# Eight head transposes on SyncE's DMA instead of TensorE, and a new order of steps, in a fused linear-attention and gated-unit kernel

## The chip, the cores and the metric

The kernel runs on one core of one Trainium2 chip. The metric is the device time of one execution in microseconds (us), the median of several executions. The engines are named as the profile names them: PE is TensorE (PEld its weight loads), DVE is VectorE, ACT is ScalarE, POOL is GpSimd, and SP is SyncE, which here only issues DMAs and passes signals on. A name with a q, such as SPq, is the engine's instruction queue.

## What is computed

There are 8 batches of 8 heads, 576 tokens and 64 values per head. Both parts of the reference, cut to what matters:

```python
def phi(x):                                   # w_phi: 64 x 128
    proj = np.einsum('bhsd,df->bhsf', x, w_phi)
    proj = proj - np.max(np.abs(proj), axis=-1, keepdims=True)
    return np.concatenate([np.exp(proj), np.exp(-proj)], axis=-1)
q_p, k_p = phi(q), phi(k)
kv  = np.einsum('bhsf,bhsd->bhfd', k_p, v)
z   = np.sum(k_p, axis=2)
num = np.einsum('bhsf,bhfd->bhsd', q_p, kv)
den = np.einsum('bhsf,bhf->bhs', q_p, z)[..., None] + 1e-06
x   = (num / den).transpose(0, 2, 1, 3).reshape(B, S, 512)

gate_pre = sum(conv_w[k] * x_shifted_by(4 - k) for k in range(5))   # causal, along the tokens
val = x @ moe_w_val
out = (sigmoid(gate_pre) * val) @ moe_w_out
```

## The kernel before

**Units and stages.** The work is cut into 32 units, one for each pair of heads: units 0 to 3 are batch 0, and so on, so that units 20 to 23 are batch 5 and units 24 to 27 batch 6. A partition holds nine neighbouring tokens; eight of them go through the units and the ninth of all four units of a batch through a small extra unit (names that end in e). For one unit, in order:

- T (L347) transposes k and q on PE, Tc copies them out of PSUM; PK and PQA (L360) project them.
- mKa, mKb and mQ (L377, DVE) take the maxima; Ka, Kb (L441, ACT) the exponentials of k, E (L426, ACT) the factors of the maxima; V (L467, L471, POOL) scales v by them, DMQ (L412, POOL) spreads q's maxima.
- PQa and PQb (L534, PE) project q the other way round, in two halves that write one bank from different rows of the array. WQ (L526) is an empty instruction in SP's queue that waits for PQa, and PQb waits for it. SH (L550) subtracts the maxima; Qp and Qm (L564, ACT) are q's exponentials.
- KV (L488, L496, PE) sums over the tokens, KVM copies the sums; NUM (L582, PE) is numerator and denominator, RCP and XN (L597, L602, DVE) divide: XN is 128 tokens x 512 values, in bf16.
- The gated part needs XN transposed. XP (L612, PE) makes four transposes of 128 x 128 into one bank of PSUM, and XC (L152 on ACT, L154 on DVE) copies that bank into XT, the transposed x of the batch.

Once the four units of a batch are in XT, HL (L154, POOL) copies the halo of the convolution inside XT; GA (L796, PE) is the convolution, TH (L828, ACT) the gate, VA (L839) and GV (L860) the value, OUT (L868) the last product, OE (L891 on ACT, L893 on DVE) the copy out of PSUM, ST (L903, SP) the store. Two batches share one ninth-token pass (GAe to STe).

**What sets the order.** Every step is a word of one long string, `ORDER`, for instance `XP21@3` (unit 21, PSUM bank 3) or `XC21:D` (on DVE; A is ACT, P is POOL). A loop walks the string and issues the steps; each engine executes its own instructions strictly in that order, and an instruction that has to wait holds all that follow it on its engine. Semaphores between engines, buffers and DMAs are set by the framework. SP's DMAs use eight completion semaphores in turn, so a DMA on SP also waits until the eighth one before it has landed. Loads of k and q are issued by POOL, loads of v, all stores and the WQ instructions by SP.

**The second way for XC.** Where XC carries no engine letter, the step already knows another form: one DMA on SP's queue that transposes XN and writes XT, without PE, PSUM or a copy.

```python
def crossbar(i):
    u = units[i]
    nc.sync.dma_start_transpose(
        xt(u.b)[:, u.hp, 4 + u.hp % 2:12 + u.hp % 2, :].rearrange("p (j g) t -> p j (g t)", g=2),
        u.XN[:, :, :, :].rearrange("p a x d -> p (a x d)"),
    )
```

In the kernel before no step uses it.

Of the kernel before, what the change touches and what calls it, by code (L numbers as in the profile page):

```python
# [76 lines left out]
ST3_3 LVa7 LVb6 PQb22 SH22 VA4_1@2 GV4_1 Ka24 Qm22 KV22@6 KVM22:D Qp22 NUM21@0 RCP21 mKb24 E24 V24:P OUT4_1@7
PQA25@2 OE4_1:A XN21 STe1 PKe6@4 OUT4_3@0 mQ25 KTe6 OE4_3:A PQea5@6 WQe5 mQe6 DMQe6:P PK25@2,1 PQeb5 SHe5 mKe6
ST3_1 Qe5 KV23@3 T26@0 PQa23@4 WQ23 KVM23:D PQb23 SH23 mKa25 Ee6 Tc26:D Kb25 NUM22@6 RCP22 XP21@3 XN22 Qp23
Qm23 OUT4_0@0 XP22@6 XP20@7 XC21:D OE4_0:A Ka25 mKb25 NUM23@3 OUT4_2@1 DMQ25:P XC20:D RCP23 XC22:D XN23 E25  # L80
PQA26@5 OE4_2:A PK26@2,7 PQa24@3 Ka26 WQ24 NUMe5@0 PQb24 mQ26 DMQ24:P SH24 RCPe5 XNe5 Qm24 Qp24 Te7@1 Tce7:D
XP23@5 Ve6:P T27@6 XC23:D V25:P KV25@0 mKb26 KVM25:A XPe5@5 XCe5:D DMQ26:P HL5:P mKa26 Kb26 KV24@1 KVM24:D E26
V26:P LE7 PQa25@4 WQ25 PQb25 SH25 NUM24@0 Tc27:D RCP24 GA5@2,6 XN24 Qp25 Qm25 THy5 PK27@1,0 mKb27 mKa27
VA5_1@4 THx5 Ka27 NUM25@6 Kb27 VA5_0@5 RCP25 XN25 T28@3 XP24@2 PQA27@6 GV5_0 Tc28:A XP25@5 XC24:D XC25:A
PQa26@1 ST4_1 WQ26 T31@0 PQb26 SH26 Qp26 mQ27 PKe7@6 GV5_1 Qm26 mQe7 mKe7 Tc31:D VA5_2@3 GV5_2 KV26@5 KTe7
VA5_3@4 E27 DMQe7:P T29@2 GV5_3 Tc29:D GAe2@0,6 KVM26:A PK28@5,4 PQa27@2 LVb7 Ee7 ST4_3 THey2 PQA28@6 mKa28
THex2 WQ27 mQ28 DMQ27:P PQb27 SH27 Kb28 T30@0 Tc30:D OUT5_3@1 V27:P NUM26@6 Qp27 Qm27 mKb28 RCP26 Ve7:P Ka28
OUT5_1@0 KV27@2 PQea6@4 WQe6 E28 XN26 KVM27:A PK29@7,3 OE5_1:A PQeb6 SHe6 OE5_3:D mKa29 mKb29 OUT5_2@2 OE5_2:D
Qe6 NUM27@0 RCP27 Kb29 NUMe6@6 PQa28@4 RCPe6 OUT5_0@2 XN27 XP26@0 XNe6 Ka29 XC26:A OE5_0:D XP27@3 DMQ28:P
XPe6@1 XC27:D WQ28 XCe6:A PQA29@6 mQ29 E29 PQb28 SH28 Qm28 PK30@0,2 Qp28 mKb30 Ka30 VAe2@1 GVe2 V28:P KV28@3  # L90
# [932 lines left out]
```

## Time and profile before

| | |
|---|---|
| median of 3 runs | 221.36 us (219.36 to 221.43) |
| profiled execution, its own time | 220.76 us |
| its span | 219.0 us, 8941 instructions |
| granted PE clock over the span | 0.981 |
| PE busy | 201.0 us, 92% |
| ACT busy | 193.7 us, 88% |
| DVE busy | 188.0 us, 86% |
| POOL busy | 149.9 us, 68% |
| moved by DMA | 32.40 MB, mean 148 GB/s |

The span runs from the first to the last instruction that the profile shows; the time has 1.8 us more around it. Busy times count computing instructions alone. In a row of the timeline the first number is the start, the second how long the merged group took, and a bracket at the end says how long the engine had been idle and what released it. Instructions of one engine overlap a little, so what a step costs its engine is the distance from its start to the start of the next one, not its own length.

### The profile page before, as it was taken

How to read it: one execution, taken by the hardware profiler on the slowest of the kernel's cores; microseconds unless marked ns; L12 is line 12 of the kernel's file. 1: busy time of each engine (PE TensorE's matmuls, PEld its weight loads, DVE VectorE, ACT ScalarE, POOL GpSimd, SP SyncE). 2: the span in 40 equal slices, each digit the busy share in tenths (PEclk: the TensorE clock that was granted, in tenths of full speed). 3: DMA queues.
4: the chain of work that ended last, by engine and by line, in shares of the span. 5: the costliest groups of instructions: out<-in, count | busy, mean ns of one | idle time of the engine just before them, and what ended most of it. 6: DMA issues, size and time to landing. Idle time of an engine off the chain costs nothing.

```text
span 219.0 us, 8941 instructions
## 1 busy us (share of the span) xinstructions
PE 201.0 (92%) x3755; PEld 134.6 (61%) x3788; DVE 188.0 (86%) x339; ACT 193.7 (88%) x386; POOL 149.9 (68%) x180
## 2 busy tenths in 40 slices
PE   7676989979999999999999999999999999999991
PEld 2443758647676676766676668655576667656640
DVE  6786999989999999989989999898998999876362
ACT  3599899998999999999999999799999999988450
POOL 8969968999676498986864768595881695840000
PEclk9969699999999999999999999999999999999998
DMA  6999995069989912999980794719922800404726
GB/s 168 231 256 209 242 218 122 4 136 203 246 183 177 236 34 48 158 226 253 256 201 3 138 196 103 152 31 216 240 49 76 207 15 1 102 18 128 187 57 192
DMA packets 28194, 32.40 MB, mean 148 GB/s; under 512 B 6005, under 2 KB 23285, under 8 KB 28154
## 3 DMA queue, kind: packets, MB, share of 16 engines
q1 hardware_dynamic: 18282, 20.79, 38.7%
q0 software_dynamic: 9328, 10.19, 28.8%
q10 hardware_dynamic: 544, 0.85, 1.2%
q8 instruction: 29, 0.48, 0.9%
q14 instruction: 11, 0.09, 0.2%
HBM read 32.58 MB, written 9.44 MB: 192 GB/s over the span
## 4 chain that ended last, share of the span: by engine, by line
PE 67%; DMA 7%; POOL 6%; issue 5%; DVE 5%; ACT 4%; SPq 3%; POOLq 0%; DVEq 0%; ACTq 0%
PE PS L868 11%; PE PS L839 8%; DMA kN<-in_k_dram 7%; PE PS L496 7%; PE PS L582 6%; PE PS L347 5%; PE PS L360 5%; PE PS L612 4%; PE PS L534 4%; PE PS L796 3%; PE PS L550 3%; PE PS L488 2%; ACT KT L441 2%; PE PS L948 2%; POOL VT L467 2%
## 5 line engine op out<-in xcount | busy, mean ns | idle before, releaser
L467 POOL TENSOR_TENSOR VT<-vN,E 128x1024 bf16<-128x1024 f32 x32 | 61.0, 1905 | 23.3 <-ACT E L426 23.0
L441 ACT ACTIVATE KT<-PS 128x512 bf16<-128x512 f32 x128 | 69.2, 640 | 1.7 <-PE PS L360 0.9
L564 ACT ACTIVATE QT<-PS 128x1024 bf16<-128x1024 f32 x64 | 62.4, 1056 | 1.7 <-PE PS L550 1.4
L377 DVE TENSOR_REDUCE MK<-PS 128x4 f32<-128x512 f32 x64 | 42.6, 682 | 2.9 <-PE PS L360 2.2
L377 DVE TENSOR_REDUCE MQ<-PS 128x8 bf16<-128x1024 f32 x32 | 39.1, 1221 | 4.4 <-PE PS L360 3.8
L412 POOL TENSOR_TENSOR DM<-id,MQ 128x512 bf16<-128x512 bf16 x32 | 33.1, 1040 | 11.7 <-DVE MQ L377 11.4
L868 PE MATMUL PS<-WOUT,GV 128*128 128x512 bf16 x113 | 30.2, 379 | 1.2 <-issue 0.6
L839 PE MATMUL PS<-XT,WVAL 128*128 128x512 bf16 x115 | 29.9, 379 | 0.8 <-issue 0.2
L360 PE MATMUL PS<-W,T 64*128 64x128 bf16 x512 | 24.8, 222 | 2.1 <-ACT T L152 1.1
L496 PE MATMUL PS<-VT,KT 128*128 128x65 bf16 x512 | 24.0, 196 | 0.0
L860 DVE SCALAR_TENSOR_TENSOR GV<-GATE,PS 128x512 bf16<-128x512 bf16 x32 | 21.1, 682 | 3.4 <-ACT GATE L823 2.1
L360 PEld LDWEIGHTS <-T 64*128 64x128 bf16 x512 | 17.6, 97 | 9.1 <-issue 4.0
L602 DVE TENSOR_TENSOR XN<-PS,RCP 128x512 bf16<-128x512 f32 x32 | 21.9, 687 | 0.7
L496 PEld LDWEIGHTS <-KT 128*128 128x128 bf16 x512 | 21.7, 99 | 0.9
L582 PEld LDWEIGHTS <-QT 128*128 128x128 bf16 x512 | 18.4, 97 | 4.8 <-issue 2.4
L582 PE MATMUL PS<-KVS,QT 128*128 128x65 bf16 x512 | 20.8, 193 | 0.0
L534 PE MATMUL PS<-T,W 64*128 64x256 bf16 x128 | 17.8, 281 | 2.5 <-SPq L526 1.2
L154 DVE COPY T<-PS 128x1024 bf16<-128x1024 bf16 x27 | 18.2, 682 | 1.8 <-PE PS L347 1.8
L467 POOL TENSOR_TENSOR VZ<-vE,Ee 64x512 bf16<-64x512 f32 x16 | 16.6, 1039 | 2.9 <-ACT Ee L426 2.3
L839 PEld LDWEIGHTS <-WVAL 128*128 128x128 bf16 x128 | 11.2, 98 | 11.7 <-issue 0.9
L868 PEld LDWEIGHTS <-GV 128*128 128x128 bf16 x128 | 10.8, 98 | 10.8 <-issue 1.3
L488 PE MATMUL PS<-VZ,KTe 128*128 128x130 bf16 x64 | 14.3, 223 | 0.1
(92 smaller groups left out, 365.0 us busy)
## 6 DMA issues: line engine op xcount, KB each, us to landing
vN<-in_v_dram SPq DMA_DIRECT2D x32, 320.0 KB, 7.0
out_dram<-OS SPq DMA_DIRECT2D x28, 256.0 KB, 4.1
qN<-in_q_dram POOLq DMA_DIRECT2D x7, 576.0 KB, 11.4
kN<-in_k_dram POOLq DMA_DIRECT2D x7, 576.0 KB, 10.3
vE<-in_v_dram SPq DMA_DIRECT2D x16, 64.0 KB, 6.4
out_dram<-OSe SPq DMA_DIRECT2D x8, 128.0 KB, 4.8
GV<-in_moe_w_val_dram POOLq DMA_DIRECT2D x1, 512.0 KB, 16.0
WOUT<-in_moe_w_out_dram POOLq DMA_DIRECT2D x4, 128.0 KB, 13.6
```

The source lines that it names most:

```text
L360: (nc.tensor.matmul(PS[:, banks[g], jj * F:(jj + 1) * F], T[row(g), n, jj, :, :].rearrange("p a t -> p (a t)"), W2[row(g), :], start=True, ...
L377: nc.vector.tensor_reduce(dst, x, AX.X, ALU.max, apply_absolute_value=True)
L412: engines[eng].tensor_tensor(u.DM[:, :, :], id64[:, :].unsqueeze(1).to_broadcast([P, n, 64]), u.MQ[:, :, :].rearrange("p j g -> p (j g)"). ...
L441: nc.scalar.activation(u.KT[:, ft, par, :, :].rearrange("p b f -> p (b f)"), PS[:, u.PK[par], :], AF.Exp, scale=1.0 if ft == 0 else -1.0,)
L467: engines[eng].tensor_tensor(dst[:, :, :, 0:D].rearrange("p f (h m) d -> p f h m d", m=m), x.unsqueeze(1).to_broadcast(s), e.rearrange("p ...
L496: nc.tensor.matmul(o, u.KT[:, ft, y % 2, h2 * 2 + y // 2, :], u.VT[:, ft, h2 * 4 + y, :], start=False, stop=(y == 3), skip_group_check=True,)
L534: return nc.tensor.matmul(PS[:, u.PQ + a, :].rearrange("p (j g t) -> p g j t", g=2, t=64)[:, g, :, :], W2[row(g), :], u.T[row(g), 1, :, a, :],
L564: nc.scalar.activation(u.QT[:, ft, :, :, :].rearrange("p a n t -> p a (n t)"), half(u.PQ, 512), AF.Exp, scale=1.0 if ft == 0 else -1.0,)
L582: (nc.tensor.matmul(u.NUM[:, jj // 2, x * E1:(x + 1) * E1], u.QT[:, ft, jj // 2, 4 * h2 + 2 * (jj % 2):4 * h2 + 2 * (jj % 2) + 2, :].rearr ...
L602: nc.vector.tensor_tensor(u.XN[:, :, :, :], numview(u)[:, :, :, 0:D], u.RCP[:, :, :].unsqueeze(3).to_broadcast([P, 2, 4, D]), ALU.mult,)
L839: nc.tensor.matmul(PS[:, m.val[r], :], WVAL[:, dt, r, :], xt(b)[:, dt, 4:12, :].rearrange("p n t -> p (n t)"), start=(dt == 0), stop=(dt = ...
L868: nc.tensor.matmul(PS[:, m.out[j], :], m.GV[:, r, j * P:(j + 1) * P], WOUT[:, r, :], start=(r == 0), stop=(r == 3),)
```

## The change

The only edit is the string ORDER. Three things differ in it.

1. Eight steps are gone, XP20 to XP27, and the eight steps XC20 to XC27 have lost their engine letter (six were on DVE: 20 to 24 and 27; two on ACT: 25 and 26). Units 20 to 27, batches 5 and 6, thus get into XT by SP's DMA. The other 24 units keep XP and XC.
2. The whole string is written in another order, with other PSUM banks, from the first loads to the last stores.
3. Some copies have another engine. On ACT there are three more KVM (13 to 16) and three more OE (18 to 21), and fewer Tc (5 to 3), Tce (3 to 2), XC (9 to 6) and XCe (1 to 0). On DVE there are three fewer KVM (19 to 16), three fewer OE (14 to 11), two more Tc (27 to 29), one more Tce (5 to 6), five fewer XC (23 to 18) and one more XCe (7 to 8). At the start one ZV (two memsets) goes from DVE to ACT and ND from DVE to POOL; at the end HLa7 goes from ACT to POOL.

Since string and banks differ nearly everywhere, two lines of the diff show its kind:

```diff
-PQA25@2 OE4_1:A XN21 STe1 PKe6@4 OUT4_3@0 mQ25 KTe6 OE4_3:A PQea5@6 WQe5 mQe6 DMQe6:P PK25@2,1 PQeb5 SHe5 mKe6
-ST3_1 Qe5 KV23@3 T26@0 PQa23@4 WQ23 KVM23:D PQb23 SH23 mKa25 Ee6 Tc26:D Kb25 NUM22@6 RCP22 XP21@3 XN22 Qp23
...
+DMQ23:P SH23 NUM22@4 mKb25 XC21 Qp23 RCP22 XN22 V23:P E25 KV23@0 KVM23:D OUT4_2@1 OE4_2:D T26@5 Qm23 NUM23@2
+XC22 Tc26:D OUT4_0@0 V24:P Kb25 RCP23 XN23 XC23 Te7@1 PK26@7,5 PQa24@3 Ka25 Tce7:D NUMe5@6 mKa26 RCPe5 XNe5
```

Three places of the program show what moves. (Lines of the changed kernel are one lower than before.)

**SP's queue around batches 5 and 6.** vN and vE are buffers of v, OS and OSe the outputs, XT_129 the x of batches 4 and 5, XT_131 that of 6 and 7. Before, from batch 3's last stores to batch 5's (the vN pair is the last load of v):

```order
L903 DMA out_dram<-OS 64x2x512 x2
L297 DMA vE<-in_v_dram 128x2x64 x2
L903 DMA out_dram<-OS 64x2x512 x2
L292 DMA vN<-in_v_dram 64x4x320 x2
L903 DMA out_dram<-OS 64x2x512 x6
```

After, the same place:

```order
L902 DMA out_dram<-OS 64x2x512 x2
L977 DMA out_dram<-OSe 64x512 x2
L618 DMA_TRANSPOSE XT_129<-XN 128x4x128 x3
L618 DMA_TRANSPOSE XT_131<-XN 128x4x128 x2
L291 DMA vN<-in_v_dram 64x4x320 x2
L902 DMA out_dram<-OS 64x2x512 x4
L618 DMA_TRANSPOSE XT_131<-XN 128x4x128
L902 DMA out_dram<-OS 64x2x512 x2
L618 DMA_TRANSPOSE XT_131<-XN 128x4x128
```

Seven of the eight transposes stand here, between loads and stores (the eighth, unit 20's, is some DMAs earlier). Each waits in the queue for its XN on DVE, and for the DMA eight places before it. The WQ instructions, which these lists leave out, stand among them: WQ24 right behind the transposes of units 21, 22 and 23, WQ27 behind those of 24 and 25 and two loads, WQ29 behind that of unit 27 and two stores.

**DVE in batch 5.** MK is a maximum, XN the divided result, T the transposed k and q, KVS the sums. Before, from unit 22's division to the copies of batch 5:

```order
L597 RECIPROCAL RCP<-PS 128x8
L602 TENSOR_TENSOR XN<-PS,RCP 128x512
L154 COPY XT_129<-PS 128x512
L377 TENSOR_REDUCE MK<-PS 128x4
L154 COPY XT_129<-PS 128x512
L597 RECIPROCAL RCP<-PS 128x8
L154 COPY XT_129<-PS 128x512
L602 TENSOR_TENSOR XN<-PS,RCP 128x512
```

After, from the same division on:

```order
L596 RECIPROCAL RCP<-PS 128x8
L601 TENSOR_TENSOR XN<-PS,RCP 128x512
L153 CAST KVS<-PS 128x260
L892 TENSOR_SCALAR OS<-PS 128x512
L153 COPY T<-PS 128x1024
L596 RECIPROCAL RCP<-PS 128x8
L601 TENSOR_TENSOR XN<-PS,RCP 128x512
```

The three copies into XT are gone from between the divisions of units 22 and 23, and other copies stand there.

**POOL before the convolution of batch 5.** VT is scaled v, DM the spread maxima; the COPY of XT_129 onto itself is HL5. What an instruction waits for is in its bracket (DMAHW: a DMA issued by SP). Before:

```order
L467 TENSOR_TENSOR VT<-vN,E 128x16x64 [waits Activation_49,Pool_49]
L471 CAST VT<-E 128x16
L412 TENSOR_TENSOR DM<-id_138,MQ 128x512 [waits DVE_49]
L154 COPY XT_129<-XT_129 128x4x4x63 [waits DVE_49]
L467 TENSOR_TENSOR VT<-vN,E 128x16x64 [waits DMAHW7_49,DMAHW0_49,Activation_49]
```

After:

```order
L411 TENSOR_TENSOR DM<-id_138,MQ 128x512 [waits DVE_49,Pool_49]
L466 TENSOR_TENSOR VT<-vN,E 128x16x64 [waits Activation_49]
L470 CAST VT<-E 128x16
L153 COPY XT_129<-XT_129 128x4x4x63 [waits DMAHW2_49,DMAHW1_49,DMAHW5_49,DMAHW0_49,DVE_49]
L411 TENSOR_TENSOR DM<-id_138,MQ 128x512 [waits DVE_49]
L466 TENSOR_TENSOR VT<-vN,E 128x16x64 [waits DMAHW3_49,Activation_49]
```

HL5 now waits for the four DMA transposes of its batch; behind it on POOL are the spread maxima and the scaled v of unit 26. HL6 stands the same way in batch 6.

More of the change, by code (lines that the diff above doesn't have):

```diff
@@ L79 @@
-ST3_1 Qe5 KV23@3 T26@0 PQa23@4 WQ23 KVM23:D PQb23 SH23 mKa25 Ee6 Tc26:D Kb25 NUM22@6 RCP22 XP21@3 XN22 Qp23
[L80 to L88, printed above, removed]
@@ L89 @@
-Qe6 NUM27@0 RCP27 Kb29 NUMe6@6 PQa28@4 RCPe6 OUT5_0@2 XN27 XP26@0 XNe6 Ka29 XC26:A OE5_0:D XP27@3 DMQ28:P
-XPe6@1 XC27:D WQ28 XCe6:A PQA29@6 mQ29 E29 PQb28 SH28 Qm28 PK30@0,2 Qp28 mKb30 Ka30 VAe2@1 GVe2 V28:P KV28@3
-Kb30 KVM28:D PQA30@6 mQ30 PQa29@4 OUTe2@1 V29:P KV29@3 OEe2:A WQ29 mKa30 NUM28@6 E30 KVM29:A RCP28 XN28
-DMQ29:P HL6:P PQb29 SH29 Qm29 Qp29 PQA31@0 mQ31 GA6@2,6 PK31@0,1 VA6_1@4 VA6_2@5 THx6 mKa31 THy6 NUM29@2 mKb31
-XP28@6 VA6_3@7 Ka31 Kb31 GV6_2 RCP29 XN29 XC28:A V30:P ST5_3 DMQ31:P VA6_0@5 GV6_3 PQea7@2 E31 PQa31@0 WQe7
@@ L99 @@
[L99 to L100 removed]
+LVa0 IF0:D CQ0 LQa0 LE0 LKa0 CK0 T0@2 Tc0:D ZV2:A W0 ZV0:D T1@0 PQA0@6 mQ0 PK0@1,3 mKb0 Tc1:A FL15@4 LQb0
+PK1@2,0 PQA1@4 Ka0 LKb0 mKa0 FL13@6 LK1 Ka1 ND0:P FL3@6 FL8@7 mKb1 E0 Te0@6 mQ1 Tce0:D T2@7 Kb1 Tc2:D LQ1 LQ2
+mKa1 PKe0@4 PQA2@6 mQ2 Kb0 KTe0 LK2 PK2@3,1 TP0@0 CW0 LWV0 Ka2 Kb2 V0:P DMQ0:P mKe0 T3@2 Ee0 LE1 E1 PQa1@6
+mQe0 Tc3:D FL6@0 LVb0 WQ1 FL0@0 PQb1 DMQ1:P mKa2 SH1 Qm1 Qp1 LWO0 FL11@0 DMQ2:P PK3@5,2 PQa0@3 WQ0 mKa3 FL2@0
@@ new lines @@
+PQea5@0 WQe5 NUM21@4 RCP21 PQeb5 SHe5 E24 PQa23@2 WQ23 OE4_1:A KVM22:A Ee6 Qe5 PK25@6,7 XN21 mKa25 PQb23
+DMQ23:P SH23 NUM22@4 mKb25 XC21 Qp23 RCP22 XN22 V23:P E25 KV23@0 KVM23:D OUT4_2@1 OE4_2:D T26@5 Qm23 NUM23@2
+XC22 Tc26:D OUT4_0@0 V24:P Kb25 RCP23 XN23 XC23 Te7@1 PK26@7,5 PQa24@3 Ka25 Tce7:D NUMe5@6 mKa26 RCPe5 XNe5
+Ve6:P WQ24 KV24@1 T27@2 OE4_0:A PQb24 Kb26 KVM24:D SH24 Ka26 PQa25@6 Qp24 Tc27:D XPe5@2 mKb26 Qm24 PQA26@0 E26
+DMQ25:P V25:P WQ25 PQb25 SH25 Qp25 XCe5:D Qm25 KV25@2 mQ26 KVM25:D NUM24@4 HL5:P RCP24 XN24 GA5@0,2 THx5
@@ new lines @@
+PQeb6 DMQe6:P SHe6 OE5_2:D mKa29 Qe6 V28:P PK30@6,5 OUT5_3@4 NUM27@0 VAe2@7 mKb30 E29 RCP27 PQa28@2 XN27
+OE5_3:A V29:P Kb30 GVe2 PQA29@0 ST5_1 WQ28 PQb28 SH28 mQ29 Qp28 NUMe6@4 Qm28 DMQ29:P OUTe2@7 RCPe6 XNe6 KV28@1
+KVM28:A mKa30 XPe6@0 PQA30@4 XCe6:D PQa29@2 OEe2:A mQ30 XC27 NUM28@0 HL6:P Ka30 KV29@7 E30 RCP28 ST5_3 XN28
+WQ29 PQb29 KVM29:A SH29 PQA31@4 GA6@6,0 Qp29 Qm29 DMQ30:P mQ31 PK31@4,5 mKa31 mKb31 THx6 VA6_0@2 V30:P THy6
+GV6_0 DMQ31:P VA6_1@3 KV30@6 E31 GV6_1 Kb31 KVM30:D VA6_3@7 PQea7@2 WQe7 PQa30@5 WQ30 GV6_3 PQa31@0 Ka31
```

113 lines of the change are left out of this document (57 added, 56 removed).

## Prediction, made before the changed kernel ran

> **What bounds the kernel now.** I read the page first, then its share of busy time by stretches, then the chain of waits and the timeline of batches 5 and 6. Three stretches of the span, with the busy time of PE, PEld, DVE, ACT and POOL in that order, the PE clock and the DMA share:
>
> ```profile
> 0.00:25.00 25.00, 17.85 (x191) 10.45 (x193) 19.39 (x35) 17.85 (x32) 21.45 (x36) 0.89 1.07 218
> 25.00:200.00 175.00, 169.31 (x3321) 116.59 (x3348) 159.87 (x289) 168.76 (x343) 128.40 (x145) 1.00 0.67 140
> 200.00:219.00 19.00, 13.83 (x247) 7.58 (x248) 8.75 (x17) 7.05 (x14) 0.00 (x0) 0.96 0.48 126
> ```
>
> Between 25 and 200 us no single engine is the bound: PE is busy for 169.3 of 175 us (97%), ACT for 168.8 (96%), DVE for 159.9 (91%). PE's figure is of overlapping matmuls, so it could hide slack; the chain that ended last says how much of it counts:
>
> ```profile
> PE 67%; DMA 7%; POOL 6%; issue 5%; DVE 5%; ACT 4%; SPq 3%; POOLq 0%; DVEq 0%; ACTq 0%
> ```
>
> Two thirds of the chain are PE's. So time taken from PE alone would soon meet ACT, and time taken from ACT alone would meet PE: a gain needs both, and is the smaller of the two. The granted clock is 1.00 throughout the middle, so it has nothing to give there.
>
> The first 25 us wait for loads. PE stands for k and q, and ACT is full from about 8 us on:
>
> ```profile
> 12.07 0.40 PE L347 MATMUL PS<-ident,qN 128*128 128x128 bf16 x4 [1.59 <-DMA qN<-in_q_dram]
> 21.03 0.40 PE L347 MATMUL PS<-ident,kN 128*128 128x128 bf16 x4 [1.39 <-DMA kN<-in_k_dram]
> ```
>
> **The change part by part.** *PE loses eight XP.* In the timeline of PE the eight transposes of this group cost, to the start of the next group:
>
> ```profile
> 156.09 0.62 PE L612 MATMUL PS<-ident,XN 128*128 128x128 bf16 x8
> 156.54 0.66 PE L582 MATMUL PS<-KVS,QT 128*128 128x65 bf16 x16
> ...
> 167.66 0.39 PE L612 MATMUL PS<-ident,XN 128*128 128x128 bf16 x4
> 167.98 0.40 PE L360 MATMUL PS<-W,T 64*128 64x128 bf16 x8
> ```
>
> Two units take 0.45 us (0.22 each) where nothing intervenes, one takes 0.32 where the next group starts late. Eight times that is 1.8 to 2.6 us; I take 2.0, nearer the lower end, since the next group starts late only where it would wait anyway. They lie on the path: PE is what the chain runs over.
>
> *DVE loses copies.* Costs from start to start, on DVE: XT 0.33 (Te, of the same shape, is taken at that), XT's ninth tokens 0.20, KVS 0.34, OS 0.61, T 0.60:
>
> ```profile
> 160.53 0.41 DVE L154 COPY XT<-PS 128x512 bf16<-128x512 bf16 x1
> 160.86 0.68 DVE L377 TENSOR_REDUCE MK<-PS 128x4 f32<-128x512 f32 x1
> 161.45 0.28 DVE L154 COPY XT<-PS 128x256 bf16<-128x256 bf16 x1
> 161.65 0.68 DVE L377 TENSOR_REDUCE MK<-PS 128x4 f32<-128x512 f32 x1
> 162.25 0.42 DVE L154 CAST KVS<-PS 128x260 bf16<-128x260 f32 x1
> 162.59 0.68 DVE L154 COPY T<-PS 128x1024 bf16<-128x1024 bf16 x1
> ...
> 171.42 0.68 DVE L154 COPY T<-PS 128x1024 bf16<-128x1024 bf16 x1
> 172.02 1.33 DVE L860 SCALAR_TENSOR_TENSOR GV<-GATE,PS 128x512 bf16<-128x512 bf16 x2
> ...
> 180.18 0.69 DVE L893 TENSOR_SCALAR OS<-PS 128x512 f32<-128x512 f32 x1
> 180.79 0.20 DVE L597 RECIPROCAL RCP<-PS 128x8 f32<-128x8 f32 x1
> ```
>
> By the counts of the change: -5 x 0.33 - 3 x 0.34 - 3 x 0.61 + 2 x 0.60 + 0.33 + 0.20 = -2.8 us.
>
> *ACT loses a little less.* From start to start: XT 0.48, KVS 0.27, OS 0.54, T 0.90; an XT with the ninth tokens' copy behind it takes 0.75, so those cost 0.27; Te has XT's shape and is taken at 0.48.
>
> ```profile
> 135.75 0.63 ACT L152 ACTIVATE XT<-PS 128x512 bf16<-128x512 bf16 x1
> 136.23 0.65 ACT L891 ACTIVATE OSe<-PS 128x512 f32<-128x512 f32 x1
> ...
> 149.77 0.72 ACT L891 ACTIVATE OS<-PS 128x512 f32<-128x512 f32 x1
> 150.31 1.16 ACT L686 ACTIVATE KTe<-PS 128x512 bf16<-128x512 f32 x2
> ...
> 168.48 1.12 ACT L152 ACTIVATE T<-PS 128x1024 bf16<-128x1024 bf16 x1
> 169.38 0.71 ACT L152 ACTIVATE XT<-PS 128x512 bf16<-128x512 bf16 x1
> ...
> 172.97 0.41 ACT L152 ACTIVATE KVS<-PS 128x260 bf16<-128x260 f32 x1
> 173.24 0.33 ACT L426 ACTIVATE Ee<-MKe 128x4 f32<-128x4 f32 x2
> ...
> 182.38 0.87 ACT L152 ACTIVATE XT<-PS 128x512 bf16<-128x512 bf16 x2
> 183.13 0.31 ACT L426 ACTIVATE E<-MK 128x8 f32<-128x8 f32 x2
> ```
>
> By the counts: +3 x 0.27 + 3 x 0.54 - 2 x 0.90 - 0.48 - 3 x 0.48 - 0.27 = -1.6 us. The copies that moved from DVE to ACT thus eat most of what the other moves free there, and ACT is the engine that frees least. The ZV that comes to ACT at the start stands before 8 us, where ACT waits; HLa7 leaves ACT at the end, where it is busy 7.05 of 19 us. I cost both at nothing; if the cover fails, a few tenths.
>
> *SP gains eight DMA transposes.* The trace of before has none, so issue and landing are bounded by the nearest rows: a pair of plain DMAs on SP, and the median time from issue to landing of several sizes (one transpose moves 128 KB).
>
> ```profile
> 162.38 1.30 SPq L903 DMA_DIRECT2D out_dram<-OS  x2
> ...
> vN<-in_v_dram SPq DMA_DIRECT2D x32, 320.0 KB, 7.0
> out_dram<-OS SPq DMA_DIRECT2D x28, 256.0 KB, 4.1
> ...
> out_dram<-OS SPq DMA_DIRECT2D x4, 128.0 KB, 2.7
> ```
>
> Issue: 0.65 us each as a plain DMA. Landing: 2.7 us, the row of the same size, up to 7.0, the row of the slowest kind on the same queue; I take 3, near the same size, and keep 7.0 for the range. On the data path that is well above XP and XC (0.22 to 0.32 and 0.33 to 0.48 us), so what matters is what covers it. In batch 5 the last transpose follows XN23; behind XN23 ACT's new order still has Ka25, OE4_0, Kb26, Ka26 and the two exponentials of unit 24 before NUM24 and GA5 can run. With a pair of k exponentials at 0.97 us and a pair of q exponentials at 1.81, this is 3 x 0.97 + 0.54 + 1.81 = 5.3 us:
>
> ```profile
> 158.71 1.08 ACT L441 ACTIVATE KT<-PS 128x512 bf16<-128x512 f32 x2
> 159.68 1.95 ACT L564 ACTIVATE QT<-PS 128x1024 bf16<-128x1024 f32 x2
> 161.49 0.42 ACT L152 ACTIVATE KVS<-PS 128x260 bf16<-128x260 f32 x1
> ...
> 161.80 1.02 POOL L154 COPY XT<-XT 128x1008 bf16<-128x1008 bf16 x1 [0.45 <-DVE XT L154]
> ```
>
> The need is 0.65 + 3 + 1.02 (HL5 on POOL) = 4.7 us: hidden, with little to spare. Batch 6 has a similar list between XN27 and GA6 (OE5_3, Kb30, the exponentials of unit 28, OEe2, Ka30). So I cost latency at nothing, and between 0 and 3.4 us a batch (8.7 with the 7.0 landing, less 5.3). Loads are nearly over by then, so bandwidth does not enter. Queued behind a waiting transpose on SP are WQ24, WQ27 and WQ29: PE's second half PQb waits for those, and Qp, Qm on ACT behind it. Such waits exist already, small:
>
> ```profile
> PEld L534 <- SPq L526: 3.1, 6, 1.6
> ```
>
> [...]
>
> *The new order and banks.* They have no row. Before, ACT is idle for 175 - 168.8 = 6.2 us of the middle and PE for 5.7; a perfect list would win those, a worse one can lose as much. I take nothing, for want of a reason for either sign. At the start T0 moves ahead of three filler and tap groups on PE, but the product PQA0 stands behind T1, which waits for a load as before; and the waits at 12.07 and 21.03 are for loads that are issued in nearly the same order. I cost the start at nothing, and at half a microsecond either way.
>
> **The sum.** PE -2.0, ACT -1.6, DVE -2.8. The smaller of PE and ACT would be -1.6; some of ACT's 6.2 idle us are waits for PE, so the fall lies between: -1.9. Against the profiled execution's own time that is 220.76 - 1.9 = 218.9; that execution lies 0.6 below the median of the runs, 221.36, from which it is 219.5. I give the latter.
>
> **The rivals.**
>
> - *Nothing measurable.* The gain is swallowed by new small waits: ACT has three more KVM and OE, each of which now stands between exponentials, and POOL's HL5 and HL6 hold DMQ26 and V26, DMQ30 and V30 behind them. For it: the engines are so evenly full that each small wait counts. Against: POOL has 175 - 128 = 47 us idle in the middle. Two us of waits give 220.6 to 222.5.
> - *Slower, by late transposes.* If one lands like the loads of v (7.0 us), GA5 and GA6 wait 3.4 us each and the convolution's successors with them: 2 x 3.4 - 1.9 = +4.9, 226.3. It decides from a landing of 3.6 us, where the cover ends; at 4.6 the gain is gone (2 x 0.95), and 1% slower needs 5.7. An issue that takes longer does the same through WQ24. For it: small spare, a kind of DMA the trace doesn't have. Against: the row of the same size, 2.7. Range 222.5 to 226.3, middle 224.
> - *Better than the sum.* The new list also closes half of ACT's 6.2 idle us: 221.36 - 1.9 - 3.1 = 216.4. For it: there is a stretch where the chain leaves PE for POOL and DVE with ACT idle 1.32 us; against: nothing else says that the list is tighter.
>
> ```profile
> 139.63 0.60 ACT L891 ACTIVATE OS<-PS 128x512 f32<-128x512 f32 x1 [1.32 <-PE PS L868]
> ```
>
> **How the numbers follow.** Forecast 0.42 (218.2 to 220.6), nothing measurable 0.18, slower by late transposes 0.20, better than the sum 0.20. About 1% is what a measurement of this kernel can tell from no change: below 219.15 is faster, above 223.57 slower. Of the forecast's 0.42 a good two fifths (0.18) lie below 219.15; with the better case that makes 0.38 faster. Slower is 0.20, and the rest, 0.42, within 1%. The range reaches from the better case's 216.4 to the middle of the slower case, 224, and leaves out about 2 in 10.
>
> **What would show it.** Right: L612 with 96 matmuls in place of 128; XT copies 18 on DVE and 6 on ACT; ACT's and DVE's busy time down by about 1.6 and 2.8 us in the middle; DMA_TRANSPOSE rows on SP of some 0.65 us that land in about 3; no idle time of PE before L796 on a DMA. Wrong: PE or POOL waiting for XT from a DMA, PEld of L534 waiting for L526 by more than the 3.1 us of before, ACT's idle time in the middle above 6 us, or a span that shrinks by far more than 2 us, which the eight transposes could not explain.

## The result and the profile after

The changed kernel takes 217.96 us, the median of 3 runs (217.02 to 218.51), beside 221.36 for the kernel before. The ratio is 0.9885, with a 95% interval of 0.9837 to 0.9934: faster by 1.15%. The median lies inside the predicted range (216.4 to 224.0) and 1.5 us below the predicted 219.5. The profiled execution took 217.96 us with a span of 216.2, against 220.76 and 219.0 before. (Later sets had the kernel before at 220.2 to 220.7, medians of 17 to 26 runs; microseconds worked out from ratios below are on 220.4.) Ratios count fast executions alone: two of the six of the old list with SP's transposes (225.5 and 225.8 us) and four of the twelve of batch 4 by SP as well (220.3 to 222.8 us) were slow and are left out, and as the profiled ones are among them, the rows of these two traces say less than the others.

The three stretches that the prediction began with, in the changed kernel, with the same columns:

```profile
0.00:25.00 25.00, 18.77 (x212) 10.56 (x212) 18.18 (x35) 18.90 (x37) 19.57 (x33) 0.93 1.07 213
25.00:200.00 175.00, 171.31 (x3405) 116.10 (x3399) 159.77 (x289) 168.53 (x341) 130.74 (x150) 1.00 0.75 150
200.00:216.20 16.20, 10.48 (x172) 5.36 (x155) 4.64 (x7) 5.00 (x10) 0.31 (x1) 0.90 0.44 114
```

The middle looks as it did: PE, ACT and DVE are as full as before, the stretch of 175 us only gets further in the program. Fixed times hide where the gain is. The start of GA, the convolution of a batch, is a better mark, since it is the same step in both kernels. Here is the span cut at GA of batches 0, 4 and 6 and at its end. The kernel before:

```profile
0.00:39.99 39.99, 31.80 (x468) 21.61 (x470) 33.92 (x66) 32.29 (x65) 34.01 (x50) 0.91 0.97 198
39.99:140.25 100.26, 97.17 (x1908) 66.48 (x1923) 93.25 (x166) 96.13 (x198) 77.27 (x89) 1.00 0.80 160
140.25:188.37 48.12, 46.79 (x920) 31.89 (x929) 44.06 (x78) 47.20 (x97) 32.70 (x37) 1.00 0.42 102
188.37:219.00 30.63, 25.24 (x467) 14.64 (x468) 16.78 (x31) 18.05 (x30) 5.87 (x6) 0.97 0.43 114
```

The changed kernel, cut at the same steps:

```profile
0.00:40.72 40.72, 32.29 (x488) 21.40 (x489) 33.28 (x64) 34.62 (x72) 35.12 (x52) 0.96 1.06 212
40.72:139.43 98.71, 97.61 (x1915) 66.55 (x1914) 91.42 (x164) 95.23 (x195) 77.85 (x90) 1.00 0.80 155
139.43:184.86 45.43, 45.05 (x890) 29.49 (x889) 42.54 (x74) 44.69 (x93) 30.38 (x35) 1.00 0.70 151
184.86:216.20 31.34, 25.62 (x472) 14.59 (x468) 15.36 (x30) 17.90 (x30) 7.27 (x8) 0.95 0.34 86
```

By stretch: +0.7, -1.6, **-2.7**, +0.7, in sum -2.8. The -2.7 lie between GA of batch 4 and GA of batch 6, where the eight transposes are. In that stretch ACT is idle for 48.12 - 47.20 = 0.92 us before and 45.43 - 44.69 = 0.74 after: its length is ACT's work, which fell by 2.51. PE is as full there (46.79 of 48.12 before, 45.05 of 45.43 after). Over the whole span ACT works 1.2 us less (193.66 to 192.44) and is idle 1.6 us less, and it does 2.3 us more before GA of batch 0 (32.29 to 34.62), where it had stood idle for 7.7 us. Of the -1.6 between GA of batch 0 and of batch 4, most may be chance: in the kernel before, PE once waits 1.23 us for SP there (for WQ, at 48.4 us), and in none of the other three traces with the old list does it wait for SP in that part.

The new operation, by its tile in the changed kernel:

```profile
L618 SPq DMA_TRANSPOSE XT<-XN x8: 1191/1214/1306, 138.2 to 180.0; - x8
...
  POOL XT L153: 0.5, 1
...
DMA to landing us min/median/max: 2.4/3.4/5.8
```

An issue holds SP's queue for 1.21 us, twice the 0.65 of a plain DMA. Landing takes 3.4 us in the median, and the only one that waited for it was POOL's halo copy, once, for 0.5 us. PEld's wait for the relays (the WQ instructions in SP's queue), 3.1 us before, is smaller now although transposes stand in the same queue:

```profile
PEld L533 <- SPq L525: 1.1, 3, 0.4
```

The chain that ended last has moved from PE (67% before) to all three engines:

```profile
PE 52%; DVE 19%; ACT 17%; issue 4%; POOL 3%; DMA 3%; POOLq 0%; ACTq 0%; DVEq 0%
```

### The profile page after: what moved, and what is told of

Read it like the earlier page. It is cut to its first block, busy times and chain, and to the rows that moved or that the text cites. A ratio compares the mean times of both kernels' runs of the same rounds, so it can differ in the third digit from the quotient of the medians.

```text
span 216.2 us, 8931 instructions
## 1 busy us (share of the span) xinstructions
PE 200.6 (93%) x3756; PEld 132.0 (61%) x3756; DVE 182.6 (84%) x329; ACT 192.4 (89%) x386; POOL 150.6 (70%) x182
## 2 busy tenths in 40 slices
DMA packets 32545, 33.44 MB, mean 155 GB/s; under 512 B 10357, under 2 KB 27637, under 8 KB 32506
## 4 chain that ended last, share of the span: by engine, by line
PE 52%; DVE 19%; ACT 17%; issue 4%; POOL 3%; DMA 3%; POOLq 0%; ACTq 0%; DVEq 0%
PE PS L867 9%; PE PS L838 8%; DVE MQ L376 5%; ACT KT L440 5%; PE PS L581 5%; DVE MK L376 5%; ACT QT L563 5%; PE PS L359 4%; PE PS L795 4%; PE PS L495 4%; PE PS L346 4%; DMA kN<-in_k_dram 3%; PE PS L533 3%; DVE T L153 2%; ACT GATE L827 2%
## 5 line engine op out<-in xcount | busy, mean ns | idle before, releaser
L563 ACT ACTIVATE QT<-PS 128x1024 bf16<-128x1024 f32 x64 | 63.1, 1061 | 0.7 <-PE PS L549 0.5
L867 PE MATMUL PS<-WOUT,GV 128*128 128x512 bf16 x128 | 32.0, 379 | 0.0
L838 PE MATMUL PS<-XT,WVAL 128*128 128x512 bf16 x128 | 31.7, 380 | 0.0
L359 PE MATMUL PS<-W,T 64*128 64x128 bf16 x512 | 25.6, 223 | 1.3 <-DVE T L153 0.7
L359 PEld LDWEIGHTS <-T 64*128 64x128 bf16 x512 | 17.7, 97 | 10.2 <-issue 6.2
L495 PE MATMUL PS<-VT,KT 128*128 128x65 bf16 x512 | 23.5, 194 | 0.0
L495 PEld LDWEIGHTS <-KT 128*128 128x128 bf16 x512 | 21.2, 98 | 1.0
L153 DVE COPY T<-PS 128x1024 bf16<-128x1024 bf16 x29 | 19.5, 683 | 1.9 <-PE PS L346 1.9
L346 PE MATMUL PS<-ident,kN 128*128 128x128 bf16 x128 | 12.6, 222 | 2.9 <-DMA kN<-in_k_dram 1.9
```

The lines of the kernel that those rows point to most:

```text
L153: engines[eng].tensor_copy(dst, x)
L359: (nc.tensor.matmul(PS[:, banks[g], jj * F:(jj + 1) * F], T[row(g), n, jj, :, :].rearrange("p a t -> p (a t)"), W2[row(g), :], start=True, ...
L495: nc.tensor.matmul(o, u.KT[:, ft, y % 2, h2 * 2 + y // 2, :], u.VT[:, ft, h2 * 4 + y, :], start=False, stop=(y == 3), skip_group_check=True,)
L563: nc.scalar.activation(u.QT[:, ft, :, :, :].rearrange("p a n t -> p a (n t)"), half(u.PQ, 512), AF.Exp, scale=1.0 if ft == 0 else -1.0,)
L838: nc.tensor.matmul(PS[:, m.val[r], :], WVAL[:, dt, r, :], xt(b)[:, dt, 4:12, :].rearrange("p n t -> p (n t)"), start=(dt == 0), stop=(dt = ...
L867: nc.tensor.matmul(PS[:, m.out[j], :], m.GV[:, r, j * P:(j + 1) * P], WOUT[:, r, :], start=(r == 0), stop=(r == 3),)
```

## The experiments

Four questions: does the gain come from the eight transposes or from the new list; does the new list need them gone; what is their work worth; and how much cover do SP's transposes have? Below, "the stretch" is the time from GA of batch 4 to GA of batch 6; each row is a kernel's row for it, with the columns as above.

### The transposes and the list, apart

**The changed kernel once more**, beside the next three on one chip. Expected:

> The changed kernel once more, beside the others of this set: both theories expect the ratio to the kernel before that was measured already, 0.9885 with an interval of 0.9837 to 0.9934, about 218.4 against 221. It is the mark against which the other runs of the set are read.

Measured: 217.67 us, ratio 0.9882 (0.9837 to 0.9927), the stretch 45.45 us. The result repeats.

**The new list with TensorE's transposes.**

```diff
-XC20 ... XC27
+XP20@2 XC20:D  XP21@1 XC21:D  XP22@1 XC22:D  XP23@0 XC23:D
+XP24@4 XC24:D  XP25@5 XC25:A  XP26@0 XC26:A  XP27@0 XC27:D
```

> The new list and its banks, but the eight heads of batches 5 and 6 are transposed on TensorE and copied out of PSUM, six copies on DVE and two on ACT, as in the kernel before; SP issues no transpose. Theory A (the gain comes from the eight matmul groups and eight copies that left PE, DVE and ACT): the gain goes back, +1.9 to +2.7 us on the changed kernel, 220.0 to 221. Theory B (the gain comes from the new order and banks): within 0.5 us of the changed kernel, about 218.

Measured: 224.56 us, ratio 1.0191 (1.0150 to 1.0232). That is 6.8 us above the changed kernel, three times theory A's figure, and slower than the kernel before. The row of its stretch, and what PE waited for in it (total, times, longest):

```profile
140.30:191.82 51.52, 46.95 (x910) 31.47 (x916) 44.48 (x80) 46.36 (x95) 30.27 (x34) 1.00 0.44 111
```

```profile
PE PS L611 <- ACT KT L440: 1.8, 2, 1.3
PE PS L867 <- DVE XT L153: 0.9, 1, 0.9
PE PS L611 <- DVE MQ L376: 0.7, 1, 0.7
```

The matmuls of XP (L611) wait for banks that ACT and DVE are still reading, and another product waits for a bank that an XT copy holds. ACT is idle for 51.52 - 46.36 = 5.2 us in place of 0.7.

**The old list with SP's transposes.**

```diff
-XP21@3 XN22 ... XP22@6 XP20@7 XC21:D ... XC20:D RCP23 XC22:D
+XC21 XN22 ... XC22 XC20 ... RCP23
```

(and so for units 23 to 27: XC without a letter where XP stood)

> The old list and its banks, with only the eight transposes changed: SP issues each of them at the place in the list at which TensorE made it, and the eight copies are left out. Theory A: most of the gain is there, -1.5 to -2.8 us on the kernel before, 218.5 to 219.8. Theory B: no gain, within 0.5 us of the kernel before; and if SP's queue now holds up the relays of q and of e behind it, slower than that by up to 2 us.

Measured: ratio 1.0149 (1.0091 to 1.0206), 3.3 us *slower* than the kernel before. Theory A falls here, and theory B's "no gain" comes out with the loss that it allowed for. So neither half of the change gains anything alone. The old list gets slower with SP's transposes, the new list gets slower without them, and only both together are faster. The row of its stretch, and what PE waited for longest in it:

```profile
140.30:191.80 51.50, 46.90 (x888) 30.77 (x896) 42.71 (x72) 46.44 (x95) 32.76 (x37) 0.97 0.57 115
```

```profile
PE PS L532 <- SPq L524: 1.7, 2, 1.3
```

**The new list with no transposes at all.**

```diff
-XC20 ... XC27
```

> The new list with the eight transposes of batches 5 and 6 left out, on every engine: the projection reads what the buffers held from earlier batches, so these two batches' output is not what the reference gives; every other instruction stands where it did. It shows what the eight transposes on SP still cost. Both theories that the transposes are hidden: within 0.5 us of the changed kernel, 217.9. The rival that they come late, with 1.21 us of SP each and landings of 2.4 to 5.8 us: 1 to 3 us faster than the changed kernel.

Measured: ratio 0.9894 (0.9863 to 0.9925), the same as the changed kernel, and its stretch has the same length to the hundredth:

```profile
141.16:186.59 45.43, 44.27 (x882) 29.48 (x889) 42.53 (x75) 44.69 (x93) 30.64 (x35) 1.00 0.50 128
```

In the new list SP's eight transposes cost nothing. (The kernel leaves the eight out on every engine, so the output of batches 5 and 6 is not the reference's.)

### What the work of the eight is worth

**TensorE's transposes, better placed.** In the new list again, with other banks and places:

```diff
-XC20 ... XC27
+XP20@7 XC20:D  XP21@4 XC21:D  XP22@2 XC22:D  XP23@3 XC23:D
+XP24@3 XC24:D  XP25@6 XC25:A  XP26@5 XC26:A  XP27@5 XC27:D
```

> As the run with TensorE's transposes in the new list, but each matmul group is put in the middle of the longest stretch in which a bank lies free after its head is ready, and its copy is put before that stretch ends. Theory C (the 6.8 us of the earlier placing were 2 us of work and nearly 5 us of waits for banks that were still being read): 1.9 to 2.9 us above the changed kernel, 219.6 to 220.6. Theory D (the new list loses more than the work however the eight are placed, as no engine has a gap for them): 4 us or more above, 222 or later.

Measured: ratio 1.0227 (1.0179 to 1.0275), 7.5 us above the changed kernel: theory D. The stretch is 53.92 us, in an execution 2 us above the median. PE's waits are others, but there are as many:

```profile
PE PS L359 <- ACT XT L151: 1.6, 2, 1.3
PE PS L611 <- ACT KT L440: 0.9, 1, 0.9
PE PS L611 <- ACT QT L563: 0.8, 1, 0.8
PE PS L795 <- POOL XT L153: 0.7, 1, 0.7
```

ACT works through its queue later than the list's places suggest, so a bank that is free in the list is still being read when PE comes. Two placements by hand don't prove that no placement is good.

**Eight matmul groups more** in the changed kernel, at those places, read by nobody (`+XP20@7` ... `+XP27@5`, XC20 to XC27 unchanged):

> The changed kernel, with its transposes on SP, and eight matmul groups more, at the places of the run before: they transpose the same heads into the same free banks, and nothing reads them. PE alone gets the work of the eight back. The prediction's reading, that the gain is the smaller of PE's and ACT's relief, so that PE's work alone costs what it takes: +1.8 to +2.2 us on the changed kernel. If PE is not what binds there: under +0.7.

Measured: ratio 1.0018 (0.9994 to 1.0042), +2.9 us.

**Eight copies more** (six of 0.42 us on DVE, two of 0.64 us on ACT), without the matmuls:

```diff
+def op_XD(i, bank, eng):
+    copy(eng, IDLE[eng][:, 0:n], PS[:, bank[0], 0:n])   # n = 260 on DVE, 512 on ACT
```

> The changed kernel, with its transposes on SP, and eight copies out of PSUM more, six on DVE and two on ACT, at the places of the run with the better placed transposes: they take the same time as the copies of the heads did and go to a buffer that nothing reads. DVE and ACT alone get the work of the eight back, about 2.8 and 1.3 us. The prediction's reading (ACT as full as PE): +0.8 to +1.6 us on the changed kernel. If DVE or ACT do not bind there: under +0.5.

Measured: ratio 1.0082 (1.0048 to 1.0116), +4.3 us. The rows of the stretch of these two, the matmul groups first:

```profile
139.78:188.46 48.68, 46.68 (x922) 31.25 (x920) 43.08 (x74) 45.15 (x93) 30.75 (x35) 1.00 0.66 141
```

```profile
139.08:190.09 51.01, 47.23 (x892) 30.76 (x890) 44.49 (x81) 46.36 (x95) 31.16 (x35) 0.97 0.59 134
```

Extra work on PE becomes idle time of ACT (48.68 - 45.15 = 3.5 us in place of 0.7), extra copies become waits of PE. At these places the two prices add up (2.9 + 4.3 = 7.2) to about that of the better placed transposes (7.5); in both of the dearer kernels a drop of the clock, which comes up below, is in the price. "The smaller of the two" is not how it goes. Both prices hold waits for banks: 1.7 us for the matmul groups (ACT KT 0.9, ACT QT 0.8, as in the rows above), and for the copies this:

```profile
PE PS L359 <- ACT IDLEA L151: 2.1, 2, 1.7
```

**The same work without banks and places of its own:**

```diff
-        for n, name in enumerate(("k", "q")):
+        for n, name in ([(0, "k")] if i >= 24 else []) + [(0, "k"), (1, "q")]:
...
         copy(eng, u.KVS[:, :], u.KVps)
+        if i in (26, 29):
+            copy("A", IDLE["A"][:, 0:512], PS[:, u.KVbank, 0:512])
+        elif 22 <= i <= 28:
+            copy("D", IDLE["D"][:, 0:260], PS[:, u.KVbank, 0:260])
```

> The changed kernel with the work of eight matmul groups and eight copies added again, PE, DVE and ACT together, but without a bank of its own and without a place in the list: the four k transposes of units 24 to 31 are issued twice into the same place, and behind the copy of KV of units 22 to 29 stands a second one from the same bank into a buffer that nothing reads, six on DVE and two on ACT. The prediction's sum (the work of the eight is worth 1.9 us, the smaller of PE's and ACT's part): 1.6 to 2.6 us above the changed kernel, a ratio to the kernel before of 0.996 to 1.001. Theory D (any work added to this list costs a multiple of itself, as the 7 us of the two runs with TensorE's transposes have it): 4 us or more, a ratio of 1.006 or above. If it is under 1.6, the engines' work is worth less than the sum had it, and the list more.

Measured: ratio 1.0085 (1.0052 to 1.0119), +4.4 us. The row of the stretch:

```profile
140.17:188.60 48.43, 46.37 (x915) 30.48 (x914) 44.20 (x80) 45.46 (x93) 30.55 (x35) 1.00 0.66 140
```

Of the 4.4 us, 3.0 are in the stretch; one wait of PE for a bank held by DVE, 1.2 us, is in them. Work that has no place in the list thus costs more than twice the 1.9 us of the prediction's sum, and with banks of its own about four times the 1.9. The copies here read their bank a second time and so hold it longer, and PE waits 0.4 us for one of them, so waiting for banks is in the 4.4 us too.

**The old list without the eight transposes**, on any engine:

```diff
-XP20@7 ... XP27@3
-XC20:D ... XC27:D
```

> The old list with the eight transposes of batches 5 and 6 left out, matmuls, copies and DMAs: the projection reads what the buffers held from earlier batches, so these two batches' output is not what the reference gives. It shows what the work of the eight is worth in the old list. The prediction's sum: -1.9 us on the kernel before, a ratio of 0.991. If it comes out so, the run with SP's transposes in the old list loses about 5 us through these transposes themselves, on SP's queue or by their landing; if it comes out near 1.015 as that run did, taking work out of the old list is itself what makes it slower.

Measured: ratio 1.0054 (1.0024 to 1.0085). Taking the work out, with nothing in its place, is no gain at all. Its stretch:

```profile
140.84:188.87 48.03, 45.78 (x897) 30.20 (x898) 42.42 (x72) 46.34 (x95) 32.72 (x37) 1.00 0.42 102
```

It takes 48.03 us where the kernel before took 48.12, though PE has 32 matmuls and DVE 1.6 us less to do. (PE's busy time is 1.0 us lower; the row of before has 920 matmuls beside 929 weight loads, so some are missing from that trace and the true difference is larger.) ACT's work fell by 0.86 us (six of the eight copies had been DVE's), and its idle time rose by 0.77. PE, ahead of its time, now waits for what the old list delivers when it always did: for a relay (0.7 us), for ACT's QT (0.7) and KT (0.5), of which only 0.4 us of relay stood there before.

The 1.2 us by which this kernel is slower stand elsewhere: from GA of batch 6 to the end it takes 31.83 us, 1.2 more than before, since PE pauses in the last convolution without waiting for anything the profile shows. In the timeline of PE:

```profile
206.63 0.65 PE L794 MATMUL PS<-XT,DIAG 32*32 32x512 bf16 x31
208.21 1.02 PE L794 MATMUL PS<-XT,DIAG 32*32 32x512 bf16 x49 [0.93 <-issue]
```

All three old lists without the eight matmul groups have this pause (0.9 to 1.1 us); in the other kernels no such pause after the first 20 us is above 0.2 us. This kernel has another of 0.96 us at 73.7 us, and a later kernel, the old list with the transposes behind the relays, has two of 0.56 and 0.69 us at 66 and 73 us, where their lists do not yet differ from the kernel before. Counted in weight loads and matmuls of PE, they stand at about the 1992nd instruction, twice at the 2248th and three times at the 7368th, 256 and 5,120 apart, both whole multiples of 256; no run here tests why, and the cause stays open. The ratio of 1.0054 thus holds some 1 us that may have nothing to do with the work of the eight; the length of the stretch does not.

### The cover on SP's queue

**The old list, transposes behind the relays.**

```diff
+WQ22 XC20 ... WQ23 XC21 ... WQ24 XC22 XC23 ... WQ26 XC24 XC25 ... WQ28 XC26 XC27
```

> The old list with the eight transposes on SP, but each is issued right behind a q projection's relay on SP's queue and not ahead of it: heads 20 and 21 behind the relays of units 22 and 23, heads 22 and 23 behind that of 24, 24 and 25 behind that of 26, 26 and 27 behind that of 28. Theory E (in the run that issued them where TensorE had made them, relays stood behind transposes that waited for their heads; PE ran dry for over a microsecond, and the granted clock of 0.5 that followed took some 2 us more): the loss over the old list without transposes goes, and the ratio is that run's, 1.0054, or 1.002 to 1.008. Theory F (the transposes land too late for the copies and matmuls that read them): 1.012 or above, as before, or later still, since they are issued later.

Measured: ratio 1.0192 (1.0142 to 1.0241), no better than at the old places. Theory E falls as it was put: the transposes no longer stand ahead of the next relay, but the 1.2 us of each push the loads and stores that follow, and a later relay behind those came too late. Theory F's number comes out, but not by its mechanism alone: POOL waited 1.4 us for a landing, PE 2.2 us for a relay. PE's row:

```profile
153.98 0.23 PE L698 MATMUL PS<-Te,W 64*128 64x128 bf16 x2 [2.24 <-SPq L524]
```

What such a gap costs is more than its length. The same place in steps of 2 us; the number behind the five busy times is the granted PE clock:

```profile
150.00:152.00 2.00, 1.74 (x22) 0.80 (x21) 1.70 (x3) 2.00 (x5) 1.84 (x1) 1.00 1.02 237
152.00:154.00 2.00, 0.02 (x2) 0.02 (x4) 0.87 (x2) 0.04 (x1) 1.91 (x5) 1.00 0.98 274
154.00:156.00 2.00, 2.00 (x29) 1.84 (x30) 0.43 (x2) 1.64 (x6) 1.25 (x2) 0.56 1.09 238
156.00:158.00 2.00, 1.90 (x24) 0.79 (x23) 1.19 (x2) 0.87 (x3) 1.94 (x4) 0.59 1.08 308
158.00:160.00 2.00, 1.41 (x23) 0.75 (x19) 1.50 (x3) 2.00 (x3) 0.17 (x2) 1.00 1.15 258
```

PE is dry for 2 us, and then its clock is at one half: 0.56 and 0.59 in two steps are 1.76 + 1.64 = 3.4 us at 0.50, a loss of up to 1.7 us more. In the eight copies more, where PE had 2.1 us of waits in a row, it is the same 3.4 us:

```profile
178.00:180.00 2.00, 0.34 (x5) 0.15 (x4) 1.29 (x2) 1.97 (x7) 0.57 (x1) 1.00 0.51 108
180.00:182.00 2.00, 1.58 (x20) 0.90 (x19) 0.69 (x1) 1.73 (x6) 1.81 (x3) 0.96 0.94 231
182.00:184.00 2.00, 2.00 (x28) 2.00 (x26) 0.90 (x2) 1.48 (x3) 1.82 (x2) 0.50 0.05 14
184.00:186.00 2.00, 2.00 (x35) 1.27 (x34) 1.43 (x2) 0.38 (x1) 0.00 (x0) 0.69 0.00 0
```

The old list with SP's transposes and the better placed TensorE transposes have one such drop each in the stretch, the next kernel has two. Kernels whose gaps were shorter (1.2 and 1.3 us at most, in the same work without banks and the first placing) have none. The gaps ahead of the drops were 1.3 to 2.7 us long (the longest single waits of PE in these kernels' traces).

The length of one gap does not decide: one of 1.3 us in the better placed transposes (L359, for ACT's XT) had a drop behind it, one of 1.3 us in the first placing (L611, for ACT's KT) had none. In the traces of the kernel before and of the changed one the changes of the granted clock lie 1, 2, 56 and 59 times 3.41 us apart, and what differs between the two gaps is PE's busy time within one step of such a grid. First the step with the gap and the step behind it in the better placed transposes, then the two steps over which the gap of the first placing reaches:

```profile
181.15:184.56 3.41, 1.85 (x23) 1.10 (x22) 1.69 (x4) 3.41 (x10) 1.92 (x2) 1.00 0.76 205
184.57:187.98 3.41, 3.41 (x32) 2.58 (x31) 1.53 (x3) 2.14 (x6) 2.70 (x4) 0.50 0.00 1
```

```profile
178.56:181.97 3.41, 2.39 (x27) 1.15 (x26) 3.31 (x8) 3.41 (x8) 2.46 (x5) 1.00 0.74 233
181.97:185.38 3.41, 3.01 (x52) 2.32 (x51) 1.70 (x4) 3.11 (x10) 2.81 (x3) 1.00 0.60 148
```

In the one PE was idle for 1.56 us of its step, in the other for 1.02 and 0.40 us of two steps. The steps at full clock in the traces of the kernel before and of the changed one agree: half the clock followed those with 1.80, 1.85 and 3.26 us idle (before) and with 2.47 and 2.65 (changed), and none of those with less, which had at most 1.23 us idle (before) and 1.21 (changed). Where between 1.23 and 1.80 us the border lies, or whether it is sharp, the one case of 1.56 does not show.

**Each transpose twice** in the changed kernel, the second into a buffer that nothing reads:

```diff
+        nc.sync.dma_start_transpose(TWICE[:, i % 2, :, :], u.XN[:, :, :, :].rearrange("p a x d -> p (a x d)"))
```

> The changed kernel with each of its eight transposes issued twice, the second into a buffer that nothing reads, right behind the first on SP's queue. Since leaving all eight out changed nothing, the transposes have cover: with 1.21 us more of SP and its transfer for each, still within 0.7 us of the changed kernel if the cover on SP is over 2.4 us a batch; +1 to +3 us if the relays behind them come late.

Measured: ratio 1.0215 (1.0175 to 1.0255), +7.3 us, far beyond the 1 to 3. PE's wait for relays, and its stretch:

```profile
PE PS L533 <- SPq L525: 5.4, 4, 2.6
```

```profile
140.34:193.52 53.18, 47.77 (x890) 31.14 (x888) 43.20 (x74) 45.04 (x93) 29.99 (x34) 0.94 0.70 142
```

PE runs dry for 5.4 us behind relays, and the clock drops twice. The landings are no later (2.9 us in the median, 5.5 at most). So the cover on SP holds 1.2 us for each transpose and not 2.4: they cost nothing, and stand close to an edge.

**Batch 4 by SP as well.**

```diff
-XP16@1 ... XC16:D ... XP17@2 ... XP18@7 XC17:D ... XC18:D ... XP19@5 ... XC19:D
+XC16 ... XC17 ... XC18 ... XC19
```

> The changed kernel with the four heads of batch 4 transposed by SP's DMA as well, issued where TensorE made them; the four matmul groups and the four copies, all on DVE or ACT by their letters, are left out and nothing else of the list is moved. Theory A (work that leaves PE and the copying engines pays by itself): half of the eight heads' relief, -0.7 to -1.4 us, 216.5 to 217.3. Theory G (it pays only in a list that was laid out without it, as leaving the eight out of the old list bought nothing): within 0.5 us of the changed kernel, or slower by 1 us and more where a relay now stands behind a transpose that waits for its head.

Measured: ratio 0.9883 (0.9853 to 0.9912), as the changed kernel: theory G. Four matmul groups and four copies less buy nothing. (Its profiled execution was 2 us longer than its median; in it GA of batch 4 waited for the last landing.) No kernel here beats the changed one.

### All of them in one table

Idle is the length of the stretch less ACT's busy time in it, from the rows above and their like.

| kernel | ratio to before | stretch, us | ACT busy | ACT idle | PE clock in it |
|---|---|---|---|---|---|
| before: old list, TensorE | 1 | 48.12 | 47.20 | 0.92 | 1.00 |
| changed: new list, SP | 0.9885 | 45.43 | 44.69 | 0.74 | 1.00 |
| new list, no transposes | 0.9894 | 45.43 | 44.69 | 0.74 | 1.00 |
| new list, TensorE | 1.0191 | 51.52 | 46.36 | 5.16 | 1.00 |
| the same, better placed | 1.0227 | 53.92 | 46.25 | 7.67 | 0.97 |
| changed + matmul groups | 1.0018 | 48.68 | 45.15 | 3.53 | 1.00 |
| changed + copies | 1.0082 | 51.01 | 46.36 | 4.65 | 0.97 |
| changed + both, no banks | 1.0085 | 48.43 | 45.46 | 2.97 | 1.00 |
| changed, transposes twice | 1.0215 | 53.18 | 45.04 | 8.14 | 0.94 |
| old list, SP | 1.0149 | 51.50 | 46.44 | 5.06 | 0.97 |
| old list, SP behind relays | 1.0192 | 51.07 | 46.55 | 4.52 | 0.97 |
| old list, no transposes | 1.0054 | 48.03 | 46.34 | 1.69 | 1.00 |

Between the kernel before and the changed one the difference is ACT's work. In the others that work lies between (44.7 to 46.6 us), and what differs is how long ACT stands idle: under 1 us only in the kernel before, in the changed one, and where the changed one's transposes are left out.

One way through the table goes in single steps: 48.12 us before, 48.03 with the eight taken out of the old list, 45.43 in the new list without them, 45.43 with SP's transposes put in. On this way the whole 2.7 us come with the new list; on the way over the new list with TensorE's transposes (51.52) they come with the change to SP. So the gain can't be shared out between the two parts.

## Why the prediction was right, and where it was not

The time and the sign came out: the ratio was forecast at 219.5 / 221.36 = 0.9916 and is 0.9885, at the border between "within 1%" (0.42) and "faster by over 1%" (0.38). The reason that carried them was half of the truth.

1. **The bound: right.** PE and ACT are both full in the middle, and extra work on either side alone costs time (+2.9 and +4.3 us).
2. **"A gain needs both, and is the smaller of the two": failed as a rule for time.** It presumes that an engine with less to do ends sooner. In the old list without the transposes it does not: the rule gave -1.9 us (for ACT's 0.86 in the stretch alone it would have been -0.9), the stretch shrank by 0.1, since PE's and ACT's relief turned into waits for relays and for each other. In the new list the same work, put back, costs 4.4 us and not 1.9, and 6.8 to 7.5 with banks to find. The two engines' prices add up.
3. **The sum, -1.9: near, by another way, and so in part by luck.** The span fell by 2.8. Of ACT's -2.5 in the stretch only some 0.9 are the two copies of heads that ACT had there. ACT also has the ninth tokens' copy (DVE's now) and one OE less there, 0.8 us at the prediction's prices; the remaining 0.8 us are not accounted for. The 2.3 us more before GA of batch 0 are other work: the ZV from DVE (1.3 us), two k exponentials, one KVM and two E.
4. **"The new order and banks: nothing, for want of a reason": the step that failed.** Old list against new with SP's transposes in both: 1.0149 against 0.9882, 5.9 us. Without the eight in both, so without any part of them in the way: 1.0054 against 0.9894, 3.5 us, of which 2.6 are in the stretch. (The old lists of both pairs hold the unexplained pause of about 1 us.) The rival "better than the sum" named the mechanism (the list closes part of ACT's idle time) and overrated it: ACT's idle time fell by 1.6 us in the whole span, not by 3.1, and not in the middle, where it is 6.5 us of 175 after 6.2.
5. **Issue: mis-sized.** 0.65 us was taken, it is 1.21. Landing, taken at 3, is 3.4 (2.4 to 5.8). The landing is near that of plain DMAs, 2.8 to 3.9 us for the stores of the changed kernel; the issue, beside their 0.65, is not. At 1.21 the need of 4.7 us becomes 5.6 with the landing's median, over the cover of 5.3: by its own sum the prediction would have expected small waits, and POOL's one wait of 0.5 us is of that size.
6. **Hidden latency: right, in the new list only.** The transposes cost nothing there. The fear for the relays WQ24, WQ27 and WQ29 did not come true in the changed kernel, but it was the right fear: in both old lists with SP's transposes, and with each issued twice, PE runs dry behind relays. The rival "slower, by late transposes" priced this at up to 4.9 us by landings; what happened where it happened was the queue, and the clock behind it, and cost 3.3 to 7.3 us.
7. **The start: near its bound.** GA of batch 0 came at 40.72 after 39.99, 0.7 us later where half a microsecond either way was allowed; the repeated run had it at 39.51.
8. **The signs foretold.** XP has 96 matmuls left, and XT's copies are 18 on DVE and 6 on ACT, as said:

```profile
L611 PE MATMUL PS<-ident,XN 128*128 128x128 bf16 x96 | 8.5, 220 | 0.1
```

```profile
L153 DVE COPY XT<-PS 128x512 bf16<-128x512 bf16 x18 | 7.3, 415 | 0.7 <-PE PS L611 0.6
L151 ACT ACTIVATE XT<-PS 128x512 bf16<-128x512 bf16 x6 | 3.8, 639 | 1.6 <-DVE RCPe L745 1.5
```

Busy times "down in the middle" could not show: a fixed window of a full engine is full before and after. Two signs of being wrong came as well: POOL waited for an XT from a DMA, by 0.5 us, and ACT's idle time in the middle was above 6 us, which could tell nothing, since it was 6.2 before.

## What to carry to other kernels

In a list written out in full for several full engines, the work of a step has no price of its own: taken out it may give nothing, put in it may cost several times its length, so an edit and the order laid out for it have to be judged, and tried, as one. Compare traces between the same steps of the program, and read the bound engine's idle time there. On a queue that also passes signals, count every issue at its own length (here 1.21 us for a transposing DMA, 0.65 for a plain one), and watch PE's idle time: here 1.56 us of it within a step of 3.41 us was followed by 3.4 us at half the clock, 1.23 us was not.

## What was not expected of the hardware

A transposing DMA of 128 x 512 bf16 values between on-chip buffers holds SP's queue for 1.19 to 1.31 us in the changed kernel and adds some 540 packets under 512 bytes (10,357 in place of 6,005 for eight). A gap of PE of 1.3 to 2.7 us was followed, within two microseconds of its end, by 3.4 us at a granted clock of 0.50; the least idle time within one step of 3.41 us that had half the clock behind it was 1.56 us (the better placed transposes), less than half of the step. And in three kernels PE paused for 0.6 to 1.1 us in the midst of a group of matmuls without any wait that the profile shows, at places 256 and 5,120 of its instructions apart.
